# A gated mix of local attention and a GEGLU network: the second half's keys and queries in seven block products

## The chip, the core and the metric

The kernel runs on one core of a Trainium2 chip. Its engines are TensorE (PE; its weight loads stand as PEld), VectorE (DVE), ScalarE (ACT), GpSimd (POOL) and SyncE (SP, which here only issues DMA transfers). The metric is the device time of one execution in microseconds, as the median of several runs; less is better.

## What is computed

```python
def _A_ref(x, wqkv, wo):
    B, S, D = x.shape                 # 1, 2048, 512
    H = 32; Dh = D // H               # 16
    W, dil = 8, 2
    ...
    pos = jnp.arange(S)
    off = jnp.arange(W) * dil
    idx = pos[:, None] - off[None, :]
    ...
    logits = jnp.einsum("bhsd,bhswd->bhsw", q, kg) * scale
    ...
    attn = _softmax(logits, axis=-1)
    o = jnp.einsum("bhsw,bhswd->bhsd", attn, vg)
    return (...) @ wo

def _B_ref(x, w_gate, w_up, w_down):
    return (_gelu(x @ w_gate) * (x @ w_up)) @ w_down     # 512 x 1792, twice, and 1792 x 512

g = _sigmoid((x * gate_w).sum(-1, keepdims=True))
return g * a + (1 - g) * b
```

Each token attends to itself and to seven earlier tokens, two apart, in 32 heads of 16 channels; beside that runs a gated feed-forward network (FFN), and a gate per token mixes the two. Everything is float32.

## The kernel before

**Two parities.** The dilation is 2, so even and odd tokens never meet. They are two halves, "parities", of 1024 tokens (two blocks of four tiles of 128 tokens). The kernel computes parity 0, then parity 1: projections of keys, queries and values, the FFN in 14 chunks of 128 hidden columns (`ffn`, `gate_up`, `down`), the attention, and the output projection at the very end (`out_first`, `finish`).

**Float32 by parts.** Every operand of TensorE is split into a high and a low part in a shorter format: ScalarE copies the high part, VectorE subtracts it from the raw data for the low part. A product is three products: high by high, low by high, high by low.

**Seven products for eight.** A product of two matrices of two by two blocks can be had from seven block products in place of eight, with sums of blocks as operands (s1 to s4 of x, t1 to t4 of the weights). The FFN's gate and up products do so in each chunk (`product`, L490, seven calls in `gate_up`). The keys and queries of parity 0 do so too, in `start()` (L842 on, on the helper `block`, L941): U = a11 b11; a copy V of it takes a12 b21; then Z = s1 t1, U + s2 t2, Z + s4 b22, U + s3 t3, U + a22 t4, and sums of them on VectorE (`join`, L1008). Parity 1 takes the direct way: `project(1, 0)` (L221) computes the keys and queries of the first half of the heads, 8 tiles of 12 products; `project_one` (L251) those of the second half, in pieces beside chunks 0 and 1 of the second FFN; `project(1, 1)` the values (and the gate's sum) between the two. For parity 0 the values go beside chunks 0 and 1 (`values`, L242).

**The turn.** The end of the first FFN and what follows: the last group of `down` (8 results, L547 to L550, each scaled by ScalarE into one of three `s` buffers and stored to `out` from GpSimd's queue), the splits of x (`again`, L612) and of weights (`split_kq`, `load_cb`), the sums of x (`sums_x`, L124), the projections, and the loads for the second FFN.

**Attention.** `attention()` (L367) is a generator that works through 8 units of 128 channels (4 for each parity) almost wholly on VectorE: `scores` (L285), `softmax` (L301), `mix` (L320). Keys, queries and values pass through HBM (`ks`, `qs`, `vs`), as does the mixed output (`os`). The other code calls `pull(budget)` at many places and so lets the generator emit about that many microseconds of work; `need` makes it wait until a projection is done. `kq`, `v` and `prod` have one buffer each.

**Order.** A planner orders the instructions on each engine ahead of time by priority and modelled times; on the chip each engine then runs in that fixed order and waits for semaphores. What `pull` emits has its priority lowered (`BEHIND`). `paced` ties an instruction to the last product before it, `ordered` fixes an order on one engine, and the `Row` objects (L822) fix the order of a whole row of calls. DMA queues are in order as well: SP's carries most transfers, ScalarE's some stores, GpSimd's the stores of L550 and the accumulating transfers that make low parts of FFN weights (L453, L482).

**Buffers.** TensorE accumulates in eight PSUM banks, acc0 to acc3 and four named p. SBUF tiles rotate by name: A 6, S 8, g0 2, g1 2, d 4, raw 2, hh 6, hl 6, c 4, s 3, r 2, rt 4.

Of the kernel before, what the change touches and what calls it, by code (L numbers as in the profile page):

```python
# [33 lines left out]
FILLERS = 2  # L34
BEHIND = 150
# [12 lines left out]
def tile_gated_mix(ctx: ExitStack, tc: tile.TileContext, xt, wqkv, wff, wo, out):  # L48
# [66 lines left out]
    def split_x(par, blk, kc, cols=((0, 512),), copy=None, eng=nc.vector):  # L115
        if blk and kc < 2:
            X[par, blk, kc] = tl("rt", F32R), tl("rt", F32R)
        hi, lo = X[par, blk, kc]
        raw = XR[kc % 2][:, (2 * blk + kc // 2) * 512:]
        for a, n in cols:  # L120
            c = slice(a, a + n)
            split(eng, hi[:, c], lo[:, c], raw[:, c], copy)

    def sums_x():  # L124

        for n in ("s1", "s2", "s4", "s3"):
            for kc in range(2):
                XOP[n, kc] = pair("S")
        for kc in range(2):
            a11, a12, a21, a22 = (XR[kc][:, i * 512:(i + 1) * 512] for i in range(4))  # L130
            nc.vector.tensor_tensor(a22, a21, a22, op=OP.add)
            nc.vector.tensor_tensor(a21, a11, a21, op=OP.subtract)
            nc.vector.tensor_tensor(a11, a22, a11, op=OP.subtract)
            nc.vector.tensor_tensor(a12, a12, a11, op=OP.subtract)
            for n, x in ("s1", a22), ("s2", a11), ("s4", a12), ("s3", a21):
                split(nc.vector, *XOP[n, kc], x)
                yield

    def rooms():

        def of(*tags):
            for tag, n in tags:
                t = tl(tag, F32R)
                w = 512 if n == 4 else WA
                yield from (t[:, i * w:(i + 1) * w] for i in range(n))
        cols = of(("g1", 4))
        for _ in range(2):
            yield next(cols), next(cols)
        for _ in range(2):
            yield pair("S")  # L150
        cols = of(("g0", 3), ("g1", 3), ("c", 1), ("c", 1))
        for _ in range(KC):
            yield next(cols), next(cols)
        for _ in range(KC):
            yield pair("d")

    def load_kq_weights(raw, kc):
        nc.sync.dma_start(raw[:, :512], wqkv[0, kc // 2, :, kc % 2 * 512:kc % 2 * 512 + 512])

    def held(o, i):  # L160
        return paced(nc.scalar.activation(o, i, AF.Copy))

    def load_cb(cb, kc, tag, room, late=False):
        hi, lo = WC[cb, kc] = next(room)
        raw = tl(tag)
        n = 512
        if cb == 1:
            nc.sync.dma_start(raw[:, :CU], wqkv[1, 2, :, kc * WQ:kc * WQ + CU])
            nc.sync.dma_start(raw[:, CU:CU + WQ], wqkv[0, 2, :, kc * WQ:(kc + 1) * WQ])
            n = CU + WQ  # L170
        else:

            queue = nc.scalar if cb == 0 and kc < 2 else nc.sync
            queue.dma_start(raw[:, :n], wqkv[cb // 2, kc // 2, :, kc % 2 * 512:kc % 2 * 512 + 512])
        return lambda: split(nc.vector, hi[:, :n], lo[:, :n], raw[:, :n], held if late else None)
# [4 lines left out]
    names = iter(["acc0", "acc1", "acc2", "acc3", *["p"] * 4])  # L180
# [27 lines left out]
    def take(ps, par, jj, hh, vals, tag=None):  # L208
        st = tl(tag or next(stages))[:, :512]
        n = CU if vals else 512  # L210
# [5 lines left out]
        if not vals:  # L216
            queue.dma_start(rows(QS[par, hh], jj), two[:, 1])
        elif not hh:
            nc.scalar.activation(z[:, par, jj:jj + 1], ps[:, CU:CU + 1], AF.Copy)
# [22 lines left out]
    def values(jj):  # L242
# [5 lines left out]
        if jj == NP - 1:  # L248
            done.add((0, 1))

    def project_one(par, jj):  # L251
# [5 lines left out]
        if jj == NP - 1:  # L257
            done.add((par, 2))
# [912 lines left out]
```

## Time and profile before

| | us |
|---|---|
| median of 3 runs | 605.22 (605.12 to 605.59) |
| the profiled run | 605.68 |
| its span, first to last instruction | 603.9 |
| granted TensorE clock, mean | 0.999 |

The profile is that of one execution. "Busy" of PE is modelled from the starts of pipelined products; what tells is the idle time before a row and what released it. A row of the chain of waits gives start, length and what it is; a row of the timeline gives start, length, engine, line, operation, output and input tiles, shape and count, and in brackets the idle time before it with its releaser. In the table of stretches each engine has its busy time and, in brackets, its instructions; then come the granted clock, the mean busy share of the 16 DMA engines, and what they moved.

### The profile page before, as it was taken

To read this page: it belongs to the slowest core of one execution; us is meant where nothing else is said; L and a number is where in the kernel's file an instruction comes from. 1 tells how busy PE (TensorE), PEld (TensorE's weight loads), DVE (VectorE), ACT (ScalarE), POOL (GpSimd) and SP (SyncE) were. 2 spreads that over 40 slices of the span, in tenths; PEclk is the share of its full clock that TensorE was granted. 3 is DMA by queue.
4 is the path that set the end of the run, shared out by engine and by line. 5 is a ranking of instruction groups with operands and counts; after the bars stand their busy time and mean duration, and the time that the engine had idled before them with its cause. 6 is when DMAs were issued, how large, how long until landed. Compare 5 with 4: busy or idle time off the path is not lost.

```text
span 603.9 us, 8190 instructions
## 1 busy us (share of the span) xinstructions
PE 597.0 (99%) x2802; PEld 497.9 (82%) x2802; DVE 525.1 (87%) x611; ACT 383.4 (63%) x650; POOL 79.0 (13%) x106
## 2 busy tenths in 40 slices
PE   9999999999999999999999999999999999999997
PEld 6889977788888888878899888888888888888885
DVE  5998869999898999898989978879899999998941
ACT  6845557787678767875553356565866676677531
POOL 0501001111111111102000001111111111101200
PEclk9999999999999999999999999999999999999999
DMA  7289886999889898967889968786887768837823
GB/s 282 84 257 243 244 268 175 277 240 255 238 246 259 222 271 213 263 197 205 261 253 292 299 191 242 169 249 179 209 221 202 210 174 228 245 90 204 115 63 139
DMA packets 84741, 131.03 MB, mean 217 GB/s; under 512 B 8030, under 2 KB 52317, under 8 KB 84700
## 3 DMA queue, kind: packets, MB, share of 16 engines
q1 hardware_dynamic: 63310, 94.01, 48.2%
q0 software_dynamic: 12096, 31.40, 27.6%
q10 hardware_dynamic: 9294, 5.11, 2.8%
q8 instruction: 22, 0.36, 0.3%
q14 instruction: 19, 0.16, 0.1%
HBM read 67.18 MB, written 36.77 MB: 172 GB/s over the span
## 4 chain that ended last, share of the span: by engine, by line
PE 87%; DMA 5%; DVE 3%; ACT 3%; issue 1%; SPq 1%; DVEq 0%; ACTq 0%
PE p L495 40%; PE p L538 12%; PE acc L538 12%; PE acc L189 9%; PE p L767 5%; PE p L834 3%; PE acc L834 3%; PE p L189 2%; PE acc L767 2%; DMA kq<-qs 1%; DMA raw<-wff 1%; DVE prod L290 1%; DMA ws<-g 1%; DMA raw<-xt 1%; DMA ks<-hl 0%
## 5 line engine op out<-in xcount | busy, mean ns | idle before, releaser
L495 PE MATMUL p<-S,g 128*128 128x512 f32 x672 | 166.5, 390 | 0.1
L495 PEld LDWEIGHTS p<-S,g 128*128 128x128 f32 x672 | 125.7, 188 | 26.6 <-ACT rt L554 0.5
L495 PE MATMUL p<-A,g 128*128 128x512 f32 x504 | 127.6, 390 | 0.0
L495 PEld LDWEIGHTS p<-A,g 128*128 128x128 f32 x504 | 94.3, 188 | 19.9 <-DVE c L505 0.3
L290 DVE TENSOR_TENSOR prod<-kq 128x2048 f32<-128x2048 f32 x32 | 73.0, 2282 | 10.1 <-DMA kq<-qs 5.1
L453 POOL DMA_DIRECT2D g<-raw x40 | 34.6, 866 | 334.8 <-ACT g L452 208.1
L331 DVE TENSOR_TENSOR prod<-v,lg 128x2048 f32<-128x2048 f32 x32 | 72.9, 2277 | 5.3 <-PE acc L538 2.5
L293 DVE TENSOR_REDUCE lg<-prod 128x128 f32<-128x2048 f32 x32 | 73.0, 2283 | 0.3
L538 PE MATMUL p<-d,hh 128*128 128x512 f32 x224 | 68.1, 390 | 1.0 <-ACT hh L511 0.5
L538 PE MATMUL acc<-d,hh 128*128 128x512 f32 x224 | 62.1, 391 | 0.5 <-DVE d L87 0.5
L538 PEld LDWEIGHTS p<-d,hh 128*128 128x128 f32 x224 | 41.8, 188 | 10.5 <-ACT hh L511 0.9
L538 PEld LDWEIGHTS acc<-d,hh 128*128 128x128 f32 x224 | 41.9, 188 | 10.2 <-DVE d L87 0.9
L457 ACT ACTIVATE g<-raw 128x1024 fp32r<-128x1024 f32 (+1 forms) x40 | 39.5, 990 | 13.2 <-PE p L495 13.2
L452 ACT ACTIVATE g<-raw 128x1024 fp32r<-128x1024 f32 (+1 forms) x40 | 39.4, 985 | 5.9 <-DVE raw L434 4.8
L505 DVE TENSOR_TENSOR c<-p,s 128x512 f32<-128x512 f32 x56 | 37.9, 681 | 5.6 <-PE p L495 5.6
L509 DVE TENSOR_TENSOR c<-c 128x512 f32<-128x512 f32 x56 | 38.2, 683 | 4.9 <-ACT c L606 4.8
L538 PE MATMUL p<-d,hl 128*128 128x512 f32 x112 | 42.3, 389 | 0.0
L500 ACT ACTIVATE s<-p 128x512 f32<-128x512 f32 x56 | 33.2, 592 | 13.6 <-PE p L495 11.8
L512 DVE TENSOR_TENSOR hl<-c,hh 128x512 fp32r<-128x512 f32 x56 | 38.2, 684 | 2.7 <-ACT hh L511 2.5
L511 ACT ACTIVATE hh<-c 128x512 fp32r<-128x512 f32 x56 | 35.1, 626 | 8.4 <-DVE c L509 7.7
L335 DVE TENSOR_TENSOR prod<-prod 128x1024 f32<-128x1024 f32 x32 | 39.0, 1220 | 0.4
L554 ACT ACTIVATE rt<-p 128x512 f32<-128x512 f32 x48 | 28.1, 593 | 16.2 <-PE p L538 15.9
(193 smaller groups left out, 915.7 us busy)
## 6 DMA issues: line engine op xcount, KB each, us to landing
g<-raw POOLq DMA_DIRECT2D x27, 512.0 KB, 6.5
raw<-wff SPq DMA_DIRECT2D x42, 256.0 KB, 3.2
ws<-g SPq DMA_DIRECT2D x14, 768.0 KB, 5.6
g<-ws SPq DMA_DIRECT2D x14, 768.0 KB, 6.1
r<-wff SPq DMA_DIRECT2D x28, 256.0 KB, 3.9
d<-r POOLq DMA_DIRECT2D x26, 256.0 KB, 6.6
g<-raw POOLq DMA_DIRECT2D x13, 384.0 KB, 6.3
v<-vs SPq DMA_DIRECT2D x8, 512.0 KB, 7.6
```

The source lines that it names most:

```text
L189: LAST[:] = [nc.tensor.matmul(ps[:, :cn], a[:, t], w[:, c0:c0 + cn], start=(kc == 0 and n == 0), stop=(kc == KC - 1 and n == 2))]
L290: paced(nc.vector.tensor_tensor(prod, spans(k, jj), q[:, jj:jj + 2, None, :].to_broadcast([P, 2, W, UC]), op=OP.mult))
L293: nc.vector.tensor_reduce(two_of(lg, jj), prod.rearrange("p j w (h d) -> p (j w) h d", d=DH), axis=AX.X, op=OP.add)
L331: paced(nc.vector.tensor_tensor(prod.rearrange("p j w (h d) -> p (j w) h d", d=DH), spans(v, jj).rearrange("p j w (h d) -> p j w h d", d=D ...
L335: nc.vector.tensor_tensor(prod[:, :, :4], prod[:, :, :4], prod[:, :, 4:], op=OP.add)
L452: nc.scalar.activation(lo, raw, AF.Copy, scale=-1.0)
L457: ins = nc.scalar.activation(hi, raw, AF.Copy)
L495: LAST[:] = [nc.tensor.matmul(ps, w_, a_, start=(start and kc == 0 and n == 0), stop=(kc == 1 and n == 2), skip_group_check=True)]
L509: nc.vector.tensor_tensor(ge, ge, up, op=OP.mult)
L512: nc.vector.tensor_tensor(hl_, ge, hh_.bitcast(F32), op=OP.subtract)
L538: ins = nc.tensor.matmul(pp, a[:, ts], w, start=(i == 0 and n == 0 and gr == 0), stop=(i == 1 and n == 2), skip_group_check=True)
L767: ins = nc.tensor.matmul(pa, a, b, start=(first and n == 0), stop=(last and n == 2), skip_group_check=True)
```

## The change

The second parity's keys and queries are computed as the first parity's are, by seven block products, in a new function `kq_second()` between the two FFNs, with the operands of the first blocks made in `before()` and `ready()` at the end of the first FFN. The parts of the weight sums t1 to t4 and of the values' weights, which `start()` makes for parity 0, are stored to HBM (`store`, `keep_v`) and loaded again (`load`). The values of parity 1 move beside chunks 0 and 1 of the second FFN; the softmax of a parity's units now waits for its values. `project`, `project_one`, `sums_x`, `rooms`, `load_cb`, `load_kq_weights`, `again`, `early`, `split_kq` and `split_x` go. `pull` budgets: 2.2 for each of 24 tiles before; 1.0 (`ASK`) for each of 28 tile steps of the blocks and 2.7 for each of 8 value tiles after.

```diff
+ASK = 1.0
...
@@ attention()
+            yield from need(un[0], 1)
             yield from softmax(*un)
...
@@ before(): the last chunk of the first FFN
+        load_raw("b11", slots("g1", 4), 0, 0)
         yield
-        again(0, 0)
...
+        for k in range(2):
+            for n in "a11", "b11":
+                hi(n, k)
+                lo(n, k)
+                yield
...
@@ ffn()
-                tile_ = (lambda jj: project_one(1, jj)) if par else values
...
+                pieces = [[lambda jj=jj: values(par, jj) for jj in jjs]
+                          for jjs in (((0, 1), (2, 3), (4, 5), ()), ((6, 7), (), (), ()))[f]]
...
-                if f == 1 and not par:
+                if f == 1:
                     for g_ in range(2):
                         at(3, down_split, g_)
-                for g_ in ((), (0, 1) if par else ())[f] if f < 2 else (f,):
-                    steps = down_w(g_)
+                if f > 1:
+                    steps = down_w(f)
...
-                if f + 2 == FC:
-                    at(8, early)
+                if not f:
+                    at(5, keep_v)
...
+        else:
+            turn = ready()
         for b in range(2):
             for t in range(BT):
                 down(par, NG - 1, t, b)
...
-                if not par and not b:
-                    split_kq() if t % 2 else again(0, 1 + t)
-                elif not par and b:
-                    again(1, (2, 3, 0, 1)[t])
+                if not par:
+                    next(turn, None)
...
+    def block(ps, a, w, first, kcs=(0, 1), ask=0.0):
+        for t in range(BT):
+            for kc in kcs:
+                ah, al = OP_[a, kc]
+                wh, wl = OP_[w, kc]
+                for n, (a_, w_) in enumerate(((ah, wh), (al, wh), (ah, wl))):
+                    mm(ps[t], t, a_, w_, first and kc == 0 and n == 0, kc == 1 and n == 2)
+            if ask:
+                pull(ask)
...
+    def store(n, i, t, m):
+        nc.sync.dma_start(TS[n][i:i + m].rearrange("i p c -> p i c"), tiled(t, m))
...
+    def keep_v():
+        for kc in range(KC):
+            paced(nc.sync.dma_start(VW[kc], parts_of(VT[kc])))
...
@@ start(): behind the parts of t1 (and likewise t2; t3 in four stores; t4 in one)
+        for k in range(2):
+            store("t1", 2 * k, d_[k], 2)
...
+    def ready():
+
+        q = [[XR[k][:, i * 512:(i + 1) * 512] for i in range(4)] for k in range(2)]
+        c = lambda: slots("c", 1)
+        load_raw("b21", slots("g0", 3, WA) + c(), 0, 1)
+        load_raw("b22", slots("g0", 3, WA) + c(), 1, 1)
+        for n in ("t1", "t2"):
+            t = [tl("d", F32R) for _ in range(2)]
+            for k in range(2):
+                OP_[n, k] = t[k][:, :512], t[k][:, 512:1024]
+                load(n, 2 * k, t[k], 2)
+        yield
+        for k in range(2):
+            for n in "a12", "b21":
+                hi(n, k)
+                lo(n, k)
+            yield
...
+        for k in range(2):
+            row.tensor_tensor(s12[k], q[k][2], q[k][3], op=OP.add)
+        yield
+        both(hi, "s1")
+        both(lo, "s1")
...
+    def kq_second():
+        q, s12 = Q2["q"], Q2["s12"]
+        for i, tag in enumerate("sssc"):
+            t = tl(tag, F32R)
+            load("t3", i, t, 1)
...
+        t = tl("g1", F32R)
+        load("t4", 0, t, 4)
...
+        U = [bank(f"acc{t}") for t in range(BT)]
+        block(U, "a11", "b11", True, ask=ASK)
+        V_ = [bank("p") for _ in range(BT)]
+        for t in range(BT):
+            out_of(V_[t], U[t])
+        block(V_, "a12", "b21", False, ask=ASK)
...
+        for k in range(2):
+            sub(s12[k], s12[k], q[k][0])
+        for t in range(BT):
+            put(t, V_[t])
+        both(hi, "s2")
+        both(lo, "s2")
+        Z_ = [bank("p") for _ in range(BT)]
+        block(Z_, "s1", "t1", True, ask=ASK)
...
+        for t in range(BT):
+            out_of(p5[t], Z_[t])
...
+        block(U, "s2", "t2", False, ask=ASK)
...
+        block(Z_, "s4", "b22", False, ask=ASK)
+        both(hi, "a22", "a21")
+        both(lo, "a22", "a21")
+        for f in range(2):
+            fetch_sums(f)
+        for kc in range(KC):
+            t = tl("d", F32R)
+            WC[1, kc] = t[:, :WQ + CU], t[:, VL:VL + WQ + CU]
+            nc.sync.dma_start(parts_of(t), VW[kc])
+        steps = chain(operands(1, 0, 0), operands(1, 0, 1))
+        next(steps)
+        block(U, "s3", "t3", False, ask=ASK)
+        for t in range(BT):
+            join(1, t, Z_[t], u2[t])
+        for t in range(BT):
+            join(1, BT + t, U[t], p5[t])
+        next(steps)
+        block(U, "a22", "t4", False, ask=ASK)
+        for t in range(BT):
+            put(BT + t, U[t])
...
     keep(0)
     ffn(0)
-    for kc in range(KC):
-        load_cb(1, kc, "c", room)()
-    project(1, 0, sums_x())
-    for kc in range(KC):
-        load_cb(2, kc, "r", room, True)()
-    fetch_d(0)
-    for f in range(2):
-        fetch_sums(f)
-    project(1, 1, chain(*(operands(1, 0, i) for i in range(2))))
+    kq_second()
     ffn(1)
```

`put`, inside `kq_second`, copies a bank into an `hh` or `hl` buffer and stores keys and queries; `join` adds on VectorE and stores; all on SP's queue. Before, the first half of the heads was stored from ScalarE's queue.

More of the change, by code (lines that the diff above doesn't have):

```diff
@@ new lines, in join, with load_raw, tiled @@
+    def join(par, jj, ps, s):
+        row.tensor_tensor(s, ps, s, op=OP.add)
+        to_hbm(par, 1, jj, s)
+    TS = {n: dram.tile([4, P, 512], F32, name=f"w{n}") for n in ("t1", "t2", "t3", "t4")}
+    VW = dram.tile([KC, P, 2, WQ + CU], F32, name="wv")
+    def load_raw(n, rooms_, hh, half):
+        raw = tl("S")
+        nc.sync.dma_start(raw, wqkv[hh, half, :, :1024])
+        name(n, pairs(rooms_), halves(raw))
+    def tiled(t, n):
+        return t.bitcast(F32)[:, :n * 512].rearrange("p (i c) -> p i c", i=n)
@@ L1045, in start @@
         both(lo, "t3")
+        for i, t in enumerate(t3_):
+            store("t3", i, t, 1)
         block(U, "s3", "t3", False)
```

258 lines of the change are left out of this document (100 added, 158 removed).

## The prediction

> **What bounds the kernel now.** The page's first part comes first, for the engine without idle time; then the busy times by stretch, around the change and at the end; then the chain of waits, for the price of a block of matrix products.
>
> ```profile
> span 603.9 us, 8190 instructions
> PE 597.0 (99%) x2802; PEld 497.9 (82%) x2802; DVE 525.1 (87%) x611; ACT 383.4 (63%) x650; POOL 79.0 (13%) x106
> ```
>
> ```profile
> core 0: us, PE busy (x) PEld busy (x) DVE busy (x) ACT busy (x) POOL busy (x), PEclk, DMA share, GB/s
> 280.00:303.00 23.00, 23.00 (x107) 19.20 (x106) 23.00 (x37) 11.88 (x22) 3.15 (x6) 1.00 0.76 237
> 303.00:327.00 24.00, 24.00 (x195) 23.65 (x194) 20.42 (x22) 12.19 (x33) 0.88 (x1) 1.00 0.97 303
> 327.00:350.00 23.00, 23.00 (x103) 19.05 (x102) 22.55 (x16) 7.61 (x13) 0.87 (x1) 1.00 0.96 261
> 580.00:604.00 24.00, 20.01 (x89) 16.23 (x87) 3.88 (x6) 4.04 (x7) 0.00 (x0) 0.98 0.27 100
> ```
>
> TensorE is the bound. It is without work for 6.9 us of 603.9, and 4.0 of those lie after the last product. From 280 us, where the second parity begins, to 350 us it never stops, at full granted clock. There a product that is taken away is worth its time, and a stall costs its whole length. VectorE is full too from 280 to 303 us, and the DMA engines are at 0.97 from 303 to 327 us.
>
> ```profile
> 11.68 10.88 PE p L834 x48
> 22.56 5.44 PE acc L834 x24
> 28.00 5.44 PE p L834 x24
> 33.44 5.45 PE acc L834 x24
> 309.32 22.77 PE acc L189 x168
> 334.81 5.44 PE acc L189 x24
> ```
>
> In the chain of waits (start, length, what) 24 products of 512 columns take 5.44 us, 0.2267 us each; the half-wide ones of the values take 22.77/168 = 0.136 us. The seven-block form already stands here for the first parity (L834): its blocks follow one another with nothing between them.
>
> **The products.** For the second parity, keys and queries are now 16 tiles of 12 products, 192; seven blocks of 4 tiles with 6 products are 168. So 24 go: **-5.44 us**, and this is certain. The values' 192 half-wide products stay and only move: 26 us from before the FFN into chunks 0 and 1, in exchange for the 96 full ones of `project_one`.
>
> **VectorE and ScalarE at the turn.** Prices are these rows:
>
> ```profile
> L87 DVE TENSOR_TENSOR A<-raw,A 128x512 fp32r<-128x512 f32 x10 | 6.5, 681 | 0.0
> L614 DVE CAST A<-raw 128x512 fp32r<-128x512 f32 x6 | 2.4, 420 | 0.0
> L834 DVE TENSOR_TENSOR hh<-acc,hh 128x512 f32<-128x512 f32 x4 | 2.7, 685 | 0.1
> L834 ACT ACTIVATE p<-acc 128x512 f32<-128x512 f32 x4 | 2.0, 561 | 0.0
> ```
>
> Out go 8 casts (0.42), 28 low-part subtractions (8 of x, 12 of weights, 8 of sums) and 8 sums: 44 instructions, about 8 x 0.40 + 36 x 0.65 = 26.6 us busy. In come 22 low parts, 8 sums and 8 joins, 38 x 0.66 = 25.1 us, and 2 more in chunk 1, where `down_split` takes over from `down_w`. VectorE thus gives up almost nothing, against a TensorE with 5.4 us less. ScalarE gets 20 copies out of PSUM for 16 and 22 high parts for 20, with half its time free. I price this at 0: in the first parity the same chain ran gapless between 11.68 and 38.9 us beside a VectorE as full. Without that cover one attention instruction (2.29 us, the L331 row below) ahead of each of two late low parts costs 4.6 us; a gain has no source. Range 0 to 4.6.
>
> **The banks of block two.** This wait is new. Block one fills the four acc banks; ScalarE copies them into the four p banks, on which block two accumulates. The last down products leave the p banks only when ScalarE has scaled them (L549) into an `s` buffer. There are three buffers for eight results, each freed by its store to HBM.
>
> ```profile
> 281.07 0.68 ACT L549 ACTIVATE s<-acc,gc 128x512 f32<-128x512 f32 x1
> 281.64 1.31 ACT L549 ACTIVATE s<-p,gc 128x512 f32<-128x512 f32 x2
> 287.92 1.33 ACT L549 ACTIVATE s<-p,gc 128x512 f32<-128x512 f32 x2 [4.97 <-DMA out<-s]
> ```
>
> ```profile
> 280.23 3.34 PE L189 MATMUL acc<-g,A 128*128 128x512 f32 x14
> ```
>
> ```profile
> 282.05 1.74 POOL L550 DMA_DIRECT2D out<-s  x3 [1.60 <-ACT s L549]
> ```
>
> ```profile
> DMA to landing us min/median/max: 2.3/4.4/6.1
> ```
>
> ScalarE stands 4.97 us for that store, and is done with the third and fourth p bank at 289.25. Before, this hid behind 48 products into acc banks (to 291.1). Now block one ends at 280.23 + 5.44 = 285.67, two tiles of block two later TensorE wants the third p bank, at 288.39. It gets it at 289.25 + 0.56 = 289.81: 1.4 us late. Every bank is taken by then, so nothing can be put in between. The store that frees the buffer took 287.92 - 282.05 = 5.9 us at a DMA share of 0.79 (280 to 288 us, below); with some 3 MB of new loads beside it (b22, t1, t2, t4) the share goes towards 0.99, and 5.9 x 0.99/0.79 = 7.4 us makes it 2.9. Bounds: 0 (ScalarE's order may come out better) and 1.4 + 4.4 = 5.8 (a store twice as long as the median). I take **+2.1**, the middle of 1.4 and 2.9. [...]
>
> **The stores at the start.** The parts of t3 (four stores, 1.05 MB) go onto SP's queue just ahead of chunk 0's weights, t4 (1.05 MB) just behind.
>
> ```profile
> 33.88 0.39 SPq L423 DMA_DIRECT2D raw<-wff  x1
> 34.32 0.46 SPq L424 DMA_DIRECT2D raw<-wff  x1
> ```
>
> ```profile
> raw<-wff SPq DMA_DIRECT2D x4, 256.0 KB, 4.1
> ```
>
> ```profile
> 41.92 1.60 DVE L834 TENSOR_TENSOR raw<-raw 128x512 f32<-128x512 f32 x3
> ```
>
> ```profile
> 14.00:20.00 6.00, 6.00 (x28) 4.97 (x27) 5.56 (x8) 5.05 (x13) 2.56 (x5) 1.00 0.33 96
> 32.00:38.00 6.00, 6.00 (x28) 4.99 (x27) 5.84 (x10) 3.11 (x6) 0.00 (x0) 1.00 0.90 258
> ```
>
> The weights land at 34.32 + 4.1 = 38.4 and are wanted at 41.92: 3.5 us of slack. Four issues (1.7 us) and 1.05 MB at 258 GB/s (4.1 us) are 5.8 against it: 0 to 2.3 us late; I take **+0.4**, since the two overlap in part. The 1 MB stores of t1 and t2 begin between 14 and 24 us, where the DMA share is a third (0.33 above): nothing, and 4.1 us each if that room were gone. `keep_v`'s four stores (2.1 MB) come between 62 and 72 us, ahead of the second unit's keys on SP; late is then VectorE's attention, not TensorE.
>
> **Chunk 1's down weights.** `down_split` in place of `down_w`; in the first parity the same order cost this stall, so **+0.5** (0 to 1):
>
> ```profile
> 87.99 0.50 PE L538 MATMUL acc<-d,hh 128*128 128x512 f32 x1 [0.48 <-DVE d L87]
> ```
>
> **The sum.** 603.9 - 5.44 + 2.1 + 0.4 + 0.5 = 601.5 us of span. The profiled run took 605.68, 1.78 outside its span and 0.46 over the median of 605.22. The median becomes 605.22 - 2.4 = **602.8 us**.
>
> **Rivals.**
>
> *Full gain.* All new waits are covered, as in the first parity's gapless blocks: 605.22 - 5.44 = 599.8. Against it stands the 1.4 us of bank wait, read from times that exist already.
>
> *The turn waits for its loads (slower).*
>
> ```profile
> 272.00:280.00 8.00, 8.00 (x37) 6.61 (x36) 5.50 (x7) 5.74 (x10) 1.23 (x3) 1.00 0.72 200
> 280.00:288.00 8.00, 8.00 (x37) 6.63 (x36) 8.00 (x15) 3.03 (x7) 2.06 (x4) 1.00 0.79 246
> 303.00:318.00 15.00, 15.00 (x122) 14.74 (x121) 12.06 (x14) 8.41 (x21) 0.88 (x1) 1.00 0.96 278
> ```
>
> ```profile
> DMA packets 15144, 15.35 MB, mean 248 GB/s; under 512 B 1261, under 2 KB 12511, under 8 KB 15138
> ```
>
> From 272 to 280 us 1.6 MB moved, to 303 us another 23 x 237 = 5.45. Five of the weight loads (1.3 MB) leave; b21 and b22 (1.05), t1 to t4 (4.2) and the kept values' weights (2.1, four loads) come. So 13.1 MB have to land before the first values tile, at 280.23 + 38.1 + 1.4 = 319.7, in 47.7 us: 275 GB/s. Scaled to a full share the rows give 278 (200/0.72), 290 (278/0.96) and 311 (246/0.79), so it fits, barely. At the mean of 248 GB/s from 268 to 330 us it takes 52.8 us, 5.1 too many, and chunk 0's own 0.79 MB of weight parts another 3.2: 8.3 us, in which the bank wait is swallowed. 605.22 - 5.44 + 8.3 + 0.9 = 609.0. It decides from 5.44 - 0.9 = 4.5 us of lateness. SP's queue, which takes over 16 key and query stores from ScalarE's and can stand behind t3's wait for `s` buffers, works for it; the order of need works against it.
>
> *The bank wait doubles.* At the upper bound of 5.8 us: 605.22 - 5.44 + 5.8 + 0.9 = 606.5. The 5.9 us store speaks for it, its closeness to the maximum of 6.1 against. [...]
>
> *The attention ends too late.* The softmax of the second parity's first unit now waits for the values, which end in chunk 1.
>
> ```profile
> 358.95 2.29 DVE L331 TENSOR_TENSOR prod<-v,lg 128x2048 f32<-128x2048 f32 x1
> 576.81 0.71 DVE L344 STREAM_TRANSPOSE tb<-o 128x512 f32<-128x512 f32 x1
> 584.85 0.69 DVE L87 TENSOR_TENSOR hl<-raw,hh 128x512 fp32r<-128x512 f32 x1 [2.71 <-ACT hh L86]
> ```
>
> ```profile
> 595.09 0.61 PE L767 MATMUL p<-S,hh 128*128 128x512 f32 x2
> ```
>
> ```profile
> v<-vs SPq DMA_DIRECT2D x8, 512.0 KB, 7.6
> vs<-hh SPq DMA_DIRECT2D x8, 128.0 KB, 4.4
> ```
>
> Turn's end 320.4, chunk 0 42 x 0.2267 + 144 x 0.136 = 29.1, one product group and two tiles 7.9, store 4.4, load 7.6: the first mix begins at 369.4 instead of 358.95, 10.5 us later. The last transpose leads to operands ready at 585.5; TensorE wants them at 595.09, a slack of 9.6, less the 2.4 won: 7.2. Late by 3.3, so 606.1. Against it: the next unit's scores can fill the wait, so that I price it at 0.
>
> **Chances.** Forecast 0.38, its own range 601.0 to 604.3; full gain 0.17; loads late 0.21; bank wait doubled 0.13; attention late 0.11. A measurement tells 0.2% (1.2 us) from no change. Faster, below 604.0: nearly all of the first two, 0.53; within 0.2%: the edge of the forecast and halves of the late cases, 0.13; slower 0.34. The range runs from 599.7, the full gain, to 608.0, which takes in the last two rivals and the lighter half of the late loads (7.3 of the 8.3 us).
>
> **What would show it.** 2778 products. Right: seven L834-like blocks in 38 us plus one gap of about 2 us on p banks in the second, released by ScalarE. Wrong: a gap ahead of the first values tile or of chunk 0, released by a DMA (late loads); gaps at the sixth or seventh block, released by VectorE; idle TensorE between 580 us and the end ahead of L767; or an early gap near 44 us. If the gaps inside the span sum to over 5.4 us more than now, the forecast's sign is wrong.

## The result and the profile after

| | us |
|---|---|
| kernel before, same chip, median of 4 runs | 605.4 (605.12 to 606.35) |
| changed kernel, median of 4 runs | 624.68 (623.38 to 633.31) |
| ratio, with its 95% interval | 1.0309 (1.0287 to 1.033) |
| span of the profiled run after | 622.9, granted clock 0.991 |

The change makes the kernel 19 us slower; 602.8 was forecast. The run of 633.31 us (granted clock 0.979, in the others 0.991 to 0.994) is a slow one: the median holds it, the ratio is that of the fast runs. Line numbers from here on are those of the changed kernel unless a row is said to be of the kernel before: products of the FFN stand in L407 and L450, the rows of `start`, `ready` and `kq_second` in L726, the values' copies in L151, loads of x's raw blocks in L108, and raw weights in L795.

```profile
span 622.9 us, 8175 instructions
...
PE 598.1 (96%) x2778; PEld 495.1 (79%) x2778; DVE 525.0 (84%) x607; ACT 384.3 (62%) x653; POOL 77.5 (12%) x104
```

The page after shows 24 products fewer, as the change says, and a TensorE that is idle for 24.8 us in place of 6.9. The idle time alone is not all of it. In the table of stretches (the last three figures of a row are granted clock, DMA share and GB/s; the share adds up the times of the packets that start in the stretch, so that it can pass 1) the clock falls too. The first row is the kernel before, the others the changed one:

```profile
60.00:95.00 35.00, 34.52 (x201) 30.18 (x201) 28.05 (x28) 18.98 (x38) 2.56 (x3) 1.00 0.87 264
```

```profile
60.00:95.00 35.00, 31.18 (x183) 27.34 (x182) 24.75 (x22) 16.64 (x36) 1.71 (x2) 0.95 1.04 299
270.00:280.00 10.00, 7.38 (x33) 5.79 (x31) 5.26 (x7) 3.52 (x7) 0.00 (x0) 1.00 0.91 317
278.00:283.00 5.00, 0.00 (x0) 0.00 (x0) 4.14 (x6) 4.81 (x10) 0.00 (x0) 0.70 0.17 70
283.40:286.50 3.10, 3.05 (x7) 2.47 (x8) 3.07 (x7) 1.06 (x3) 0.00 (x0) 0.50 0.07 12
350.00:370.00 20.00, 19.11 (x144) 18.14 (x143) 10.59 (x7) 5.97 (x16) 0.00 (x0) 1.00 0.82 257
```

There are three places. Between 60 and 95 us the DMA engines are full (share 1.04, 0.87 before) and TensorE is idle for 3.8 us. From 278 to 283 us it stands still beside DMA engines that are almost idle (0.17), and then runs 3.1 us at half clock (0.50). Between 350 and 370 VectorE, the busiest engine but one, is at work for only 10.6 of 20 us.

**First place: chunks 0 and 1 of the first FFN.** Rows of the timeline after, of SP's queue, ScalarE and TensorE:

```profile
64.45 6.75 SPq L812 DMA_DIRECT2D wv<-d  x4
71.38 0.58 SPq L335 DMA_DIRECT2D raw<-wff  x1
81.91 0.32 SPq L185 DMA_DIRECT2D kq<-ks  x1
...
83.71 0.39 ACT L151 ACTIVATE c<-acc 128x256 f32<-128x256 f32 x1 [4.60 <-DMA vs<-c]
85.88 0.38 ACT L151 ACTIVATE c<-acc 128x256 f32<-128x256 f32 x1 [1.79 <-DMA vs<-c]
...
87.36 4.32 PE L407 MATMUL p<-S,g 128*128 128x512 f32 x12 [3.82 <-ACT s L412]
```

`keep_v`'s four stores hold SP from 64.45 to 71.2; the second unit's keys, loaded at 71.63 before, follow at 81.91. ScalarE stands 4.60 and 1.79 us ahead of copies of values, because the `c` buffers that they go into wait for their stores to land; behind them in its order stands the copy (L412) for which TensorE waits 3.82 us. The next 12 products take 4.32 us (granted clock 0.68 from 87.36 to 91.50 us); at 264.30, at full clock (1.00 from 264.30 to 267.00), 12 take 2.88.

**Second place: the turn.**

```profile
269.94 1.69 SPq L795 DMA_DIRECT2D S<-wqkv  x3
...
278.19 0.63 ACT L726 ACTIVATE g<-S 128x512 fp32r<-128x512 f32 x1 [5.61 <-DMA S<-wqkv]
282.81 1.63 ACT L444 ACTIVATE p<-rt 128x512 f32<-128x512 f32 x3
...
283.45 1.22 PE L450 MATMUL p<-d,hh 128*128 128x512 f32 x2 [6.07 <-ACT p L444]
```

SP can issue the raw loads of b11, b21 and b22 only at 269.94, as products up to then read the `S` buffers that the data go into (its waits there are for products of L407, the longest 2.5 us). They take 8.2 to 9.3 us to land, beside busy DMA engines (0.91 from 270 to 280 us), the first at 278.1. ScalarE's planned order has b11's high part next, so that it waits 5.61 us. It and six more high parts, with two rows of the last FFN chunk among them, then take 4.6 us, and only behind them stand the copies into p banks (L444) for which TensorE waits 6.07 us.

**Third place: the first scores of the second parity.** The first row is the kernel before, where they start without a wait, the others the changed one:

```profile
330.31 2.25 DVE L290 TENSOR_TENSOR prod<-kq 128x2048 f32<-128x2048 f32 x1
```

```profile
351.68 0.41 SPq L185 DMA_DIRECT2D kq<-ks  x1
...
359.38 2.29 DVE L201 TENSOR_TENSOR prod<-kq 128x2048 f32<-128x2048 f32 x1 [14.36 <-DMA kq<-qs]
361.70 2.29 DVE L204 TENSOR_REDUCE lg<-prod 128x128 f32<-128x2048 f32 x1
363.90 0.68 DVE L417 TENSOR_TENSOR c<-p,s 128x512 f32<-128x512 f32 x1
...
367.42 0.63 ACT L423 ACTIVATE hh<-c 128x512 fp32r<-128x512 f32 x1 [6.53 <-DVE c L421]
...
368.38 0.98 PE L130 MATMUL acc<-d,rt 128*128 128x256 f32 x6 [0.89 <-ACT c L151]
...
399.92 0.50 PE L407 MATMUL p<-A,g 128*128 128x512 f32 x1 [1.73 <-DVE c L417]
```

The first half of the heads is complete only when the seventh block is stored; its keys are loaded at 351.68. VectorE stands 14.36 us ahead of the first row of scores, then does two attention instructions, and only then the FFN's subtraction (L417). ScalarE waits 6.53 us for what follows from it, and the values' copies behind that let TensorE stop. That is 1.0 of the 5.4 us lost behind 345. Most of the rest are later waits for the same subtraction (2.6 us in three waits), the longest at 399.92: there it starts at 399.18, behind attention (L242, 2.28 us from 396.38) and L421.

In all three places one thing happens: an instruction that needs a late transfer stands, in the fixed order of an engine, ahead of work that TensorE needs now.

### The profile page after: what moved, and what is told of

Read it like the earlier page. It is cut to its first block, busy times and chain, and to the rows that moved or that the text cites. A ratio compares the mean times of both kernels' runs of the same rounds, so it can differ in the third digit from the quotient of the medians.

```text
span 622.9 us, 8175 instructions
## 1 busy us (share of the span) xinstructions
PE 598.1 (96%) x2778; PEld 495.1 (79%) x2778; DVE 525.0 (84%) x607; ACT 384.3 (62%) x653; POOL 77.5 (12%) x104
## 5 line engine op out<-in xcount | busy, mean ns | idle before, releaser
L407 PE MATMUL p<-S,g 128*128 128x512 f32 x672 | 168.3, 392 | 4.5 <-ACT s L412 3.8
L407 PEld LDWEIGHTS p<-S,g 128*128 128x128 f32 x672 | 126.1, 189 | 31.5 <-ACT s L412 4.5
L407 PE MATMUL p<-A,g 128*128 128x512 f32 x504 | 128.1, 391 | 4.1 <-DVE c L417 3.3
L407 PEld LDWEIGHTS p<-A,g 128*128 128x128 f32 x504 | 93.7, 188 | 26.3 <-DVE c L417 5.6
L450 PE MATMUL p<-d,hh 128*128 128x512 f32 x224 | 69.6, 396 | 6.1 <-ACT p L444 6.1
L242 DVE TENSOR_TENSOR prod<-v,lg 128x2048 f32<-128x2048 f32 x32 | 73.0, 2280 | 2.0 <-PE p L450 0.8
L450 PE MATMUL acc<-d,hh 128*128 128x512 f32 x224 | 60.4, 392 | 1.8 <-DMA d<-r 1.2
L450 PEld LDWEIGHTS p<-d,hh 128*128 128x128 f32 x224 | 42.7, 191 | 15.6 <-ACT p L444 6.5
L450 PEld LDWEIGHTS acc<-d,hh 128*128 128x128 f32 x224 | 42.4, 190 | 11.5 <-DMA d<-r 1.6
L450 PE MATMUL p<-d,hl 128*128 128x512 f32 x112 | 43.2, 393 | 0.0
L412 ACT ACTIVATE s<-p 128x512 f32<-128x512 f32 x56 | 33.0, 593 | 14.1 <-PE p L407 12.0
L421 DVE TENSOR_TENSOR c<-c 128x512 f32<-128x512 f32 x56 | 38.3, 683 | 3.6 <-ACT c L518 3.1
L417 DVE TENSOR_TENSOR c<-p,s 128x512 f32<-128x512 f32 x56 | 37.7, 681 | 3.3 <-PE p L407 3.3
```

What stands on the lines that cost most here:

```text
L242: paced(nc.vector.tensor_tensor(prod.rearrange("p j w (h d) -> p (j w) h d", d=DH), spans(v, jj).rearrange("p j w (h d) -> p j w h d", d=D ...
L407: LAST[:] = [nc.tensor.matmul(ps, w_, a_, start=(start and kc == 0 and n == 0), stop=(kc == 1 and n == 2), skip_group_check=True)]
L417: nc.vector.tensor_tensor(c, ps, s, op=OP.add)
L421: nc.vector.tensor_tensor(ge, ge, up, op=OP.mult)
L450: ins = nc.tensor.matmul(pp, a[:, ts], w, start=(i == 0 and n == 0 and gr == 0), stop=(i == 1 and n == 2), skip_group_check=True)
```

## The experiments

For every run the lost TensorE time was summed by place: of each product, what the distance to the next start has over 0.227 us (0.136 for the half-wide ones), where that is over 0.03. Half clock counts in it, idle time after the last product does not. The last column takes in what lies outside the others too, and is good to about 1 us.

```
us lost              30-125  250-295  295-345  345-end   all
before                  2.4      0.8      0.0      0.0    5.8
after                   8.7      7.9      1.5      5.4   28.8
e1_hold                14.2      1.1      0.7      5.6   25.7
e2_keep_one             6.8      9.5      1.3      6.4   26.2
e3_before_keep          6.7      0.8      0.0      0.0   10.4
e4_hold_keep_one        6.5      3.0      0.2      5.7   17.7
e5_kq_early             8.9      7.4      0.4      1.0   20.0
e6_keep_t1              2.7      1.7      0.4      6.4   14.9
e7_bound                2.4      8.0      0.2      0.8   15.0
e8_reload_v            10.2      1.5      6.0      1.4   22.6
e9_recompute            2.2      8.2      8.3      8.4   29.3
e10_bound_dve           2.0      1.2      0.5      0.9    7.4
e11_swap                2.2      7.7     12.8      2.0   28.4
e12_hybrid              2.3      4.4     15.1      0.9   25.8
e13_turn               11.1      0.0      1.2      7.5   24.5
e14_stores              2.1      8.2      0.9      7.0   20.5
e15_keys               13.1     10.2      1.9      6.5   36.1
e16_turn_stores         2.0      1.2      0.0      6.3   13.2
e17_all                 1.8      1.2      0.5      0.7    6.6
e18_swap                2.5      1.2      1.7      1.2    9.2
```

The first column shows that one run says little of one cause: five kernels with all the stores (after, e1, e8 without `keep_v`, e13, e15) lose 8.7 to 14.2 us there, all with few stores 1.8 to 2.7.

### e1 to e4: first pulls at the turn and at `keep_v`

```diff
# e1_hold: before() and ready()
-            for n in "a11", "b11":
-                hi(n, k)
-                lo(n, k)
-                yield
+            hi("a11", k)
+            lo("a11", k)
+            yield
...
+            paced(hi("b11", k))
+            lo("b11", k)
...
+            paced(hi("b21", k))
# e2_keep_one: keep_v() and kq_second(); e3_before_keep puts the whole keep_v() into the kernel before
-        for kc in range(KC):
-            paced(nc.sync.dma_start(VW[kc], parts_of(VT[kc])))
+        paced(nc.sync.dma_start(VW[0], parts_of(VT[0])))
...
-            nc.sync.dma_start(parts_of(t), VW[kc])
+            nc.sync.dma_start(parts_of(t), VW[0])
```

> The high parts of b11 and b21 are made two to four down tiles later, each held until the last product before it. Theory A (at the turn ScalarE stands for the load of b11, 278.1 us, with the first FFN's bank copies queued behind it in its fixed order): the 6.1 us gap at 277 to 283 us and the half clock behind it go, about 7 us in all, 624.7 to about 617 to 618; the gaps near 83 us and after 360 us stay. Rival B (the loads at the turn are late by themselves, whoever waits): a gap of 4 us or more comes back ahead of block one or two, and the time stays within 2 us of 624.7.

> Only one of the four values' weight tiles is stored to HBM beside chunk 0 (0.5 MB instead of 2.1 MB), and all four loads read that one, so parity 1's values are not the reference's. Theory C (the four stores slow the values' own stores, ScalarE waits for their c buffers, and TensorE for ScalarE's copy): the 4.0 us gap near 83 us and the half clock behind it go, 624.7 to about 619 to 620. Rival D (the t stores or the weights' fetch are to blame there): the gap stays above 2 us and the time above 623.

> The kernel before, with nothing but the four stores of the values' weights (2.1 MB) added beside chunk 0. Theory C: a gap of 2 to 4 us appears between chunks 0 and 1 (75 to 92 us), with the clock lowered behind it, 605.4 to about 609 to 611. Rival D: below 606.5.

> Both edits of e1_hold and e2_keep_one. If A and C are right and independent: both gaps go, 624.7 - 7 - 5 = about 612 to 613, with 5 us of gaps left after 360 us, which a third cause has to explain. If the two are one chain (a delay that moves on), the sum is worth less than 9 us: above 615.

Beside 604.44 of the kernel before on the same chip: e1 621.65, e2 622.62, e3 610.5, e4 614.34 us, one run each. e3 met its forecast in time: the four stores alone cost the old kernel 6 us. They do so by several waits of at most 1.44 us and not by one of 2 to 4, and its granted clock stayed at 1.00. Its rows (lines of the kernel before) show the same waits of ScalarE as after:

```profile
77.18 0.39 ACT L211 ACTIVATE c<-acc 128x256 f32<-128x256 f32 x1 [4.97 <-DMA vs<-c]
80.90 0.38 ACT L211 ACTIVATE c<-acc 128x256 f32<-128x256 f32 x1 [2.45 <-DMA vs<-c]
...
87.87 0.50 PE L538 MATMUL acc<-d,hh 128*128 128x512 f32 x1 [1.44 <-DVE d L87]
92.80 3.06 PE L495 MATMUL p<-S,g 128*128 128x512 f32 x12 [1.42 <-DVE c L505]
```

e1 and e2 fell short of what they should bring. e4 brought more than the two together and ended between its two forecasts. In e1 the turn's loss went to 1.1 us, but the first place took 14.2. One store of four was still enough for 6.5 to 6.8 us there. So `keep_v` is not the only thing that is late, and the stores ahead of it were next.

### e5 to e8: late keys, the sums' stores, all together

```diff
# e5_kq_early = e4 and: load_kq(); hh 0 of parity 1 counts as done at the end of start()
-        load_slots(k, KS[par, hh][c])
-        nc.sync.dma_start(q, QS[par, hh][c].rearrange(...))
+        src = (0, 1) if par and not hh else (par, hh)
+        load_slots(k, KS[src][c])
+        nc.sync.dma_start(q, QS[src][c].rearrange(...))
# e6_keep_t1 = e4 and: store("t2"), store("t3"), store("t4") go, load() reads TS["t1"]
# e7_bound = e4, e5 and e6
# e8_reload_v = e1 and: keep_v() goes; in kq_second(), split there by hi("v") and lo("v")
-            nc.sync.dma_start(parts_of(t), VW[kc])
+            raw = tl("c")
+            nc.sync.dma_start(raw[:, :CU], wqkv[1, 2, :, kc * WQ:kc * WQ + CU])
+            nc.sync.dma_start(raw[:, CU:CU + WQ], wqkv[0, 2, :, kc * WQ:(kc + 1) * WQ])
```

> As e4_hold_keep_one (614.34 us), but the second parity's first two attention units read keys and queries of the first parity's second half of heads, which are long in HBM, so that their scores may begin during the block products (the numbers of these units are not the reference's). Theory D: in the changed kernel the first half of the heads is complete only when the seventh block is stored, VectorE stands idle for 16 us ahead of its first row of scores at 350.75, and the attention left over then runs beside the FFN and makes TensorE wait (2.9 us at 356 to 362, 1.15 at 371, 0.86 at 449, 0.86 at 510): without it 608.5 to 610.5 us, no DVE idle time of over 3 us between 320 and 350. Rival: these waits come from the values in chunks 0 and 1 (their copies and stores): within 1.5 us of 614.3.

> As e4_hold_keep_one (614.34 us), but of the weight sums only t1's parts are stored in start(); the loads of t2, t3 and t4 read t1's (the second parity's keys and queries are not the reference's). Theory E: the 3.1 MB of stores between 20 and 45 us put SP's queue some 5 us behind (its key stores end at 48.9 in place of 45.1), and with it the FFN's loads and the values' stores, so that TensorE loses 4.0 us at 84 to 92 and 2.1 at 104 to 112 where the kernel before loses next to nothing: 609 to 611 us. Rival: one kept values' tile and the moved loads are enough for that loss: within 1.5 us of 614.3.

> The edits of e4, e5 and e6 together: the b11 and b21 parts made after the last down chunk's own work, one values' tile and t1 alone kept in HBM, the second parity's first two units reading early keys and queries. If the turn's order, the stores and the late keys are the whole of it: 603 to 606 us, close to the kernel before (604.4) less the part of the products that is not lost. If over 608 us, a cause is missing.

> A version that computes everything: the order of e1_hold (621.65 us), but the values' weights are not kept in HBM; the raw ones are loaded again at the turn and split there, four high parts on ScalarE and four low parts on VectorE (some 5 us of each). By the runs so far (e4 against e1: 7.3 us for three of the four stores) 613.5 to 616 us. If the four splits at the turn cost their own length, 618 to 620.

Beside 606.37: e5 614.95, e6 610.86, e7 609.75, e8 617.96. e6 went as theory E said: the first place fell to 2.7 us. e5 gave nothing in time, though the loss behind 345 us went from 5.7 to 1.0: the turn opened again, from 3.0 to 7.4, and the first place went from 6.5 to 8.9. e7 missed its mark for the same reason, and the row that opens its turn names the missing cause:

```profile
266.98 0.63 ACT L726 ACTIVATE A<-raw 128x512 fp32r<-128x512 f32 x1 [7.86 <-DMA raw<-xt]
```

That is the high part of a11, of x itself. In the kernel before VectorE made it (a cast in `again`); the change gave it to ScalarE, ahead of the last chunk's copies. e8 computes everything and is better than e1, but not by what was expected (613.5 to 616): it loses 10.2 us in the first place without `keep_v`: t1 to t4's stores are enough by themselves. Its new loss at the blocks is a high part of the values' weights, put on ScalarE ahead of the joins and waiting for a product; the joins' wait follows:

```profile
322.39 1.15 ACT L723 ACTIVATE d<-c 128x514 fp32r<-128x514 f32 x2 [6.75 <-PE acc L723]
...
326.08 2.09 PE L407 MATMUL p<-A,g 128*128 128x512 f32 x6 [3.73 <-DVE hl L723]
```

### e9 to e12: all three mended, and three versions that compute everything

```diff
# e10_bound_dve = e7 and, in before():
-            hi("a11", k)
+            paced(row.tensor_copy(OP_["a11", k][0], SRC["a11", k]))
             lo("a11", k)
# e9_recompute = e1 with that edit; no stores of t1 to t4, no keep_v(); raw b12, b21, b22 loaded in ready(), then
+        sub(raw["b11"], raw["b12"], raw["b11"])
...
+        sub(b11, b22, b11)
+        sub(b21, b21, b11)
+        both(hi, "t2")
+        both(lo, "t2")
...
+        sub(b12, b22, b12)
...
# e11_swap = e9 and: block(U, "a22", "t4") ahead of block(Z_, "s4", "b22"); to_hbm() with
+        queue = nc.sync if hh else nc.scalar
# e12_hybrid = e11, but t1 and t2 stored and loaded as in the change, t3, t4 and the values' weights made at the turn
```

> A version that computes everything and keeps nothing in HBM: the raw weights b12, b21, b22 and those of the values are loaded at the turn and summed and split again there, t1 to t4 by VectorE (4 sums, 8 low parts) and ScalarE (8 high parts), a11's high parts go to VectorE, b11's and b21's come after the last chunk's own work. If the stores and ScalarE's early waits are the larger part of the loss: early losses gone, the turn below 2 us, the late keys still there with their 5.7 us: 606 to 609 us. The rival: VectorE's 14 us more at the turn make TensorE wait there, or push the attention on so that the FFN pays: over 612.

> As e7_bound (609.75 us), but a11's high parts are copied by VectorE as in the kernel before, not by ScalarE. If the 7.4 us that e7 loses at 265 to 275 come from ScalarE's wait of 7.86 us for x's raw block (landing at 266.96) ahead of its work for the FFN: 603 to 605.5 us, and next to no TensorE idle time there. If that wait only hides another: over 608.

> As e9_recompute, but the product a22 t4, which completes the first half of the heads, comes sixth and s4 b22 last, and the stores of this half go on ScalarE's queue, so that the first unit's keys are loaded some 6 us earlier. If the late keys cost what e5 and e7 say (5 us for 16 us of VectorE idle): 2 to 3 us under e9. If it is the values that hold the attention, the same within 1 us.

> A version that computes everything: only t1's and t2's parts are kept in HBM (stored before 25 us, where the DMA engines are mostly idle); t3, t4 and the values' weights are summed and split again at the turn; a11's high parts on VectorE, b11's and b21's after the last chunk's own work; a22 t4 sixth, s4 b22 last, the first half of the heads stored from ScalarE's queue. If the four causes are independent of how they are removed: early losses as before, 2 us at the turn, 2 us later on: 603 to 607 us. If VectorE's 10 us more between the blocks hold TensorE, as the 14 us did in e9: 610 to 616.

Beside 605.85: e10 602.01, e9 626.06, e11 624.45; e12 in four runs 622.59 (620.98 to 624.02) beside 606.13, ratio 1.0272 (1.0243 to 1.0302). e10 went below its forecast: with a11 back on VectorE the turn loses 1.2 us, and this run, which leaves out stores and the late keys, is faster than the kernel before. The three versions that make the parts again pay at the turn what they spare at the start. e9 bears out its rival (over 612), by much more than it said. e11, 1.6 us under e9, lies between its two forecasts, and e12 above both of its own: the causes are not independent of how they are removed. In e9 ScalarE waits for VectorE's sum t1 ahead of the bank copies (L723 here):

```profile
289.72 1.15 ACT L723 ACTIVATE d<-S 128x512 fp32r<-128x512 f32 x2 [3.60 <-DVE S L723]
...
291.41 2.50 PE L723 MATMUL p<-g,A 128*128 128x512 f32 x5 [6.34 <-ACT p L723]
```

In e12 VectorE is busy without a break between 300 and 320 us, and the fifth block waits for s3 and t3:

```profile
300.00:320.00 20.00, 13.66 (x47) 10.28 (x46) 20.00 (x28) 11.48 (x22) 0.00 (x0) 0.74 0.26 84
```

```profile
310.08 0.79 PE L723 MATMUL acc<-s,S 128*128 128x512 f32 x1 [3.24 <-ACT S L723]
313.97 2.08 PE L723 MATMUL acc<-s,S 128*128 128x512 f32 x4 [3.10 <-DVE S L723]
```

### e13 to e18: one cause at a time, with repeated runs

```diff
# e13_turn = e1 with a11's cast on VectorE; e14_stores = the change with e2's and e6's edits;
# e15_keys = the change with e5's edit; e16_turn_stores = e13 and e14; e17_all = e10 again
# e18_swap = e16 and: order of the blocks s1 t1, s2 t2, s3 t3, a22 t4, s4 b22; hh 0 stored from ScalarE's queue
-        nc.sync.dma_start(rows(KS[par, hh][:, W:], jj), two[:, 0])
-        nc.sync.dma_start(rows(QS[par, hh], jj), two[:, 1])
+        queue = nc.sync if hh else nc.scalar
+        queue.dma_start(rows(KS[par, hh][:, W:], jj), two[:, 0])
+        queue.dma_start(rows(QS[par, hh], jj), two[:, 1])
```

> The changed kernel with the turn alone mended (a11's high parts on VectorE, b11's and b21's parts after the last down chunk's own work); it computes everything. If the causes add: the changed kernel's 624.7 less the 7 to 8 us that TensorE loses at 277 to 287 beyond the kernel before: 616.5 to 618.5 us. If the late stores and late keys take the time back, or scatter it: 620 to 623, as e1_hold's single 621.65 said.

> The changed kernel with the stores alone lessened: of the weight sums only t1's parts, of the values' weights only the first tile go to HBM (the second parity's numbers are not the reference's); loads and turn stay. If the causes add: less the 6 us that TensorE loses between 55 and 115 beyond the kernel before: 617.5 to 619.5. If the turn grows by as much: 622 to 625.

> The changed kernel with the late keys alone mended (the second parity's first two units read keys and queries that are early in HBM; their numbers are not the reference's). If the causes add: less the 5 us lost behind 350 us: 619 to 621. If the turn takes it back, as e5 against e4 showed in one look: 623.5 to 626.

> The turn and the stores mended, the late keys left as they are, that is e10_bound_dve (602.0 us) less its early keys. If the late keys cost 5 us by themselves: 606 to 608 us, and the kernel is no better than the one before (605.9 there) although its products are 5.4 us shorter. If they cost nothing once the rest is mended: 602 to 603.

> e10_bound_dve once more, in several rounds: turn, stores and keys mended. If the three are the whole of the loss: 601 to 603.5 us, under the kernel before, and near what the seven blocks were to give.

> e16_turn_stores (609.36 us) with the late keys mended in earnest and not by reading others: a22 t4 sixth and s4 b22 last, the first half of the heads stored from ScalarE's queue. If the 7 us between e16 and e10 are the price of some 18 us by which the keys come late, and the order wins 6 us of these: 606 to 608. If only what VectorE has to do meanwhile counts: 609 to 610.

| | us | range | ratio to before, interval |
|---|---|---|---|
| after | 624.68 | 623.38 to 633.31 | 1.0309 (1.0287 to 1.033) |
| e13, turn mended | 619.82 | 618.01 to 624.65 | 1.0237 (1.0187 to 1.0287) |
| e14, stores mended | 617.44 | 616.93 to 617.87 | 1.0185 (1.016 to 1.021) |
| e15, keys mended | 627.81 | 625.33 to 630.55 | 1.0357 (1.0316 to 1.0399) |
| e16, turn and stores | 609.36 | 608.18 to 611.98 | 1.0069 (1.0036 to 1.0102) |
| e17, all three | 602.38 | 601.11 to 604.41 | 0.9951 (0.9928 to 0.9974) |
| e18, turn and stores, blocks swapped | 605.6 | 604.08 to 607.0 | 0.999 (0.9977 to 1.0003) |

*The stores* are worth 7.2 us (after to e14). The rows that group DMA issues (the last figure is the median time to landing in us) show what mends: the values' stores, first of the kernel before, then after, then e14. Those out of the `c` buffers, which stand behind these on ScalarE's queue, took 5.1, 6.6 and 5.3 us.

```profile
vs<-hh ACTq DMA_DIRECT2D x5, 128.0 KB, 3.7
```

```profile
vs<-hh ACTq DMA_DIRECT2D x5, 128.0 KB, 8.1
```

```profile
vs<-hh ACTq DMA_DIRECT2D x5, 128.0 KB, 4.6
```

```profile
60.00:95.00 35.00, 34.80 (x203) 30.47 (x203) 29.51 (x28) 18.75 (x38) 2.56 (x3) 1.00 0.93 278
```

The last row is e14's: DMA share 0.93, TensorE 34.80 of 35 us, no less than before the change.

*The turn* is worth 8.1 us more (e14 to e16). e14, where the turn is as in the change, still has the waiting row (ScalarE, first row), e16 does not; in its stretch of 20 us (second) TensorE is idle for 0.79 us, block two's wait for a bank:

```profile
268.49 0.63 ACT L726 ACTIVATE g<-S 128x512 fp32r<-128x512 f32 x1 [5.04 <-DMA S<-wqkv]
```

```profile
272.00:292.00 20.00, 19.21 (x84) 15.41 (x83) 17.13 (x22) 14.94 (x27) 4.39 (x8) 1.00 0.82 268
```

e13 alone brought 4.9 of the 8, between the two forecasts: its turn lost nothing, but its profiled run lost 11.1 us at the first place. e15 alone ended above both its forecasts, 3.1 us over the changed kernel: behind 345 us one late load of down weights took what the keys gave (L451 is L450 of the changed kernel), and in the profiled run 13.1 us were lost at the first place and 10.2 at the turn. Why these grew is open.

```profile
407.82 2.50 PE L451 MATMUL acc<-d,hh 128*128 128x512 f32 x5 [3.87 <-DMA d<-r]
```

*The keys* are worth 7.0 us (e16, 1.4 us above its forecast, to e17), but hardly for the reason in the expectations. e18's keys come hardly earlier than e16's; what differs is what stands behind them. e16, then e18:

```profile
343.99 2.29 DVE L201 TENSOR_TENSOR prod<-kq 128x2048 f32<-128x2048 f32 x1 [14.96 <-PE acc L130]
346.31 2.29 DVE L204 TENSOR_REDUCE lg<-prod 128x128 f32<-128x2048 f32 x1
348.52 0.68 DVE L417 TENSOR_TENSOR c<-p,s 128x512 f32<-128x512 f32 x1
...
352.03 0.63 ACT L423 ACTIVATE hh<-c 128x512 fp32r<-128x512 f32 x1 [7.56 <-DVE c L421]
```

```profile
342.35 2.29 DVE L201 TENSOR_TENSOR prod<-kq 128x2048 f32<-128x2048 f32 x1 [12.82 <-DMA kq<-qs]
344.56 0.68 DVE L417 TENSOR_TENSOR c<-p,s 128x512 f32<-128x512 f32 x1
...
348.07 0.63 ACT L423 ACTIVATE hh<-c 128x512 fp32r<-128x512 f32 x1 [2.38 <-DVE c L421]
```

VectorE starts 1.6 us earlier in e18, but the FFN's subtraction stands behind one attention instruction instead of two, 4.0 us earlier in all, and e18 is 3.8 us faster. (e16's first row names a product as its releaser; its keys had landed by 343.99 at the latest, and e18's row, released by its own transfer, starts at 342.35.) That is better than the 606 to 608 expected, with keys that are at most 1.6 us and not 6 us earlier, so the theory that the price follows the keys' time does not fit. The rows suggest that it follows the number of attention rows ahead of L417. That is argued from this pair and not shown: e18 also has another order of splits and joins and another queue for these stores, and no run changes the number of rows alone.

What e17 shows is what was lost: the span less the lost time was 603.9 - 5.8 = 598.1 before and 599.5 - 6.6 = 592.9 in e17, 5.2 us less (good to some tenths). It keeps the seven blocks, all the loads and the moved values, so none of these costs much.

```profile
span 599.5 us, 8147 instructions
...
PE 592.7 (99%) x2778; PEld 493.1 (82%) x2778; DVE 523.0 (87%) x609; ACT 385.5 (64%) x652; POOL 77.4 (13%) x104
```

e17 leaves out most of the stores and the second parity's own keys; no version that computes everything came below the kernel before. The best of them is e8 with 617.96 in one run.

## Why the prediction was wrong

**The products: right.** 2778 products, and in e17 the span without lost time is 5.2 us shorter, against 5.44.

**The banks of block two: the mechanism was right, the term +2.1 too large.** The wait came in the second block, for a p bank, from ScalarE, and lasted 1.03 us (1.5 lost in all at that place, close to the 1.4 read from the old times). Right too was **chunk 1's down weights**, +0.5 against 0.58:

```profile
307.66 1.43 PE L726 MATMUL p<-g,A 128*128 128x512 f32 x5 [1.03 <-ACT p L726]
381.09 0.50 PE L450 MATMUL acc<-d,hh 128*128 128x512 f32 x1 [0.58 <-DVE d L88]
```

**VectorE and ScalarE at the turn: the step that failed, 8.1 us against a price of 0 (4.9 where it alone is mended, e13).** It counted ScalarE's 22 high parts as busy time, "with half its time free". The busy times did come out so (ScalarE 383.4 us before, 384.3 after; VectorE 525.1 and 525.0), but they were not the question. A high part that had been VectorE's cast (a11), and others whose raw data had been loaded a chunk earlier, went into ScalarE's fixed order ahead of the first FFN's bank copies; b11's raw data land at 278.1 in the changed kernel, x's at 266.98 in e7. The gapless first parity was no evidence, as there no FFN shared the engine.

**The stores at the start: the term that failed, 7.2 us against +0.4.** It asked only whether chunk 0's weights would be in time. The sums' stores lie ahead of the keys' stores on SP's queue and push it back (the last store of `start` is issued at 49.12 us, 45.11 before); those of the values' weights fall into a stretch with a DMA share of 0.87 already, which went to 1.04. What was late were the values' stores (8.1 us to landing, 3.7 before), and so the `c` buffers, and so ScalarE (4.60 and 1.79 us). The sentence on `keep_v`, that VectorE's attention would be late and not TensorE, is wrong by e3: 6 us.

**The rival "The turn waits for its loads"** had a time (609.0) on the right side, and part of its cause is there: the raw loads landed slowly beside busy DMA engines (8.2 to 9.3 us, DMA share 0.91). But its price came from the volume of loads up to 320 us, ahead of the first values tile. While TensorE stood, the DMA engines were at 0.17: it stood because of the moment of issue, at 269.94, and ScalarE's order, ahead of the blocks and not behind them. e1, with the same loads and another order, loses 1.1 us there. **"The attention ends too late"** looked at the values and at the end of the kernel, and priced the wait at 0 because "the next unit's scores can fill" it. The scores themselves were late, as the first half of the heads is complete only with the seventh block, and TensorE paid from chunk 0 on, 7.0 us from e16 to e17.

**The clock** stands in no term of the forecast's sum. After 6.07 us of idle time the stretch from 283.40 to 286.50 shows a granted clock of 0.50, and TensorE lost 1.7 us on top. Other runs show products at about half pace behind shorter waits: in e1, behind 3.25 us, twelve took 5.52 us from 102.06 to 107.58, and the next twelve 2.77; in e16, behind 1.91 us, twelve half-wide ones took 2.70 us from 352.99 to 355.69, in place of 1.42 ahead of the wait. How long TensorE has to be idle before the clock falls, and when the clock comes back, was not shown by any run.

Together: 7.2 + 8.1 + 7.0 = 22.3 us, by which e17 lies under the changed kernel (624.68 - 602.38). The order of mending matters to the single shares, as e13 and e15 show. The sign that the prediction gave for a wrong forecast came: the time lost in the span rose from 5.8 to 28.8 us, by far more than 5.4.

## What to carry to other kernels

Price an added instruction by what it waits for and by what stands behind it on its engine, not by its busy time: three moves priced at 0.4 us together cost 22 us here, through waits that the engines' fixed orders handed on. Ask of a store into HBM what else uses the DMA engines while it runs, and which buffer comes free late by it. Before mending one of several waits, mend all in one run: only e10 showed that the list of causes was complete; single mends moved the loss to another place.

## What had not been expected of the hardware

- Runs of one kernel scatter: with all stores by 6.6 us (e13) and 5.2 (e15), with few by 0.9 (e14) to 3.8 (e16), the kernel before by 3.5 beside them. That the stores are the reason is not shown.
- Four issues of 0.5 MB on SP's queue took 6.75 us after, 3.97 in e3. After, 3.3 of these lie between the first and the second, where by the trace SP waits for a store of ScalarE's queue (`vs<-hh`) to land.
- Behind waits of 3.24 and 3.10 us with one product between them (e12) eleven products took 4.86 us from 313.97 to 318.83, 0.44 us each in place of 0.227; the granted clock from 300 to 320 us was 0.74.
